# Loading and attending the first row in two halves, in a fused attention and squared-ReLU kernel

## Chip, cores and metric

One core of one Trainium2 chip. The metric is the device time of one execution in microseconds (us), lower is better; the profiled span, which the stages below are read from, is 2 to 3 us shorter than the time. The granted clock is the share of full speed that TensorE was allowed. A run is called slow when it lies over 1.5% above the fastest of the same kernel.

## The reference

```python
# q, k, v: (8 rows, 8 heads, 576 tokens, 64)
rel = pos[:, None] - pos[None, :]
mask_plain = (rel >= 0) & (rel < 32)                        # heads 0..3, "sliding"
mask_dil = (rel >= 0) & (rel < 128) & (rel % 4 == 0)        # heads 4..7, "dilated"
scores = where(mask, scale * q @ k.T, -1e9)
attn_out = softmax(scores) @ v
x = attn_out.transpose(0, 2, 1, 3).reshape(4608, 512)
r = maximum(x @ w_in, 0)                                    # w_in 512 x 2048
return (r * r) @ w_out                                      # w_out 2048 x 512
```

## The kernel before

The 4608 tokens go through the two products in nine chunks of 512; eight rows of attention feed them. Chunk 0 is special: its first product (`x @ w_in`) is cut at token 288, so that it can begin while row 0 is still being attended, and row 1 is attended between its matmuls. From chunk 1 on, round `b` runs chunk `b-1` with the attention of row `b` woven in; `pump(n)` issues `n` pieces of the pending products. `idle()` issues small useless matmuls. Row 0 (cut):

```python
    load_sliding_qk(0, (nc.sync, nc.scalar))        # q and k of row 0, one load each
    load_dilated_qk(0)
    ...
    transposes_and_scores(0, idle_and_load)         # its third call loads w_in, in two pieces
    scores_dilated(0, idle)
    ...
    load_sliding_qk(1); load_dilated_qk(1)          # row 1, behind row 0's third value product
    pending.append(mm1_part_gen(0, g0, 0, 288))     # first product of chunk 0, first part
    for a in range(2):
        pump(1); zs.append(av_dilated(0, 1, a))     # the rest of row 0 between its matmuls
    ...
    load_w_out(); pump(1000)
    pending.append(mm1_part_gen(0, g0, 288, TOKC))  # second part, between the pieces of row 1
    ...
    transposes_and_scores(1, lambda: pump(1))
    pending.append(mm2_by_rows_gen(0, g0))          # second product of chunk 0
```

The round of row 2, and the loads that all rounds share:

```python
    for b in range(2, B):
        pending.append(moe_gen(b - 1))
        pump(1)
        if 2 < b < B - 1:
            dk = keep_qk(b + 1)         # q, k of row b+1 as f16 copies, DRAM to DRAM (POOL's queue)
        ...
        for g in range(2):
            s_sliding_x(b, g); pump(5)  # needs QKTx of row b
        if b == 2:
            cast_v(nc.scalar)           # v of row 2: f32 buffers sv, sd -> f16 vp, vd
            load_v(b + 1)               # v of row 3 into the same sv, sd (SP's queue)
        s_dilated(b, 0); pump(...)
        s_dilated(b, 1)                 # needs QKTd of row b
        if b + 1 < B:
            transpose_by_dma(dk)        # DMA transposes: QKTx, QKTd of row b+1 (SP's queue)
        ...
        attn_values(b, lambda: pump(2))
```

The softmax here doesn't subtract the row's maximum and nothing guards it: scores larger than these inputs give would overflow.

## Time and profile before

| | before |
|---|---|
| time, median of 3 runs | 312.74 us (311.5 to 315.88) |
| profiled span | 310.6 us |
| first product of chunk 0 starts (on 288 tokens) | 22.9 |
| second product of chunk 0 starts | 44.8 |
| chunk 1 starts | 64.0 |
| chunk 2 starts | 99.0 |
| chunk 3 starts | 129.9 |

The starts are those of the first matmul of each stage in the timeline of TensorE. The prediction below shows the lines of chain, timeline and windows that it rests on.

```profile
98.64 0.77 POOL L394 DMA_DIRECT2D out_dram<-otl  x1 [24.20 <-DVE otl L429]
101.19 0.53 POOL L184 DMA_DIRECT2D dk<-in_k_dram  x1
```

The order: v of row 3, then the DMA transposes of row 3, all issued by 98.3 us; only then a burst on the other queue: the last stores of chunk 1 and the copies of q and k of row 4.

### The profile page before, as it was taken

To read this page: it belongs to the slowest core of one execution; us is meant where nothing else is said; L and a number is where in the kernel's file an instruction comes from. 1 tells how busy PE (TensorE), PEld (TensorE's weight loads), DVE (VectorE), ACT (ScalarE), POOL (GpSimd) and SP (SyncE) were. 2 spreads that over 40 slices of the span, in tenths; PEclk is the share of its full clock that TensorE was granted. 3 is DMA by queue.
4 is the path that set the end of the run, shared out by engine and by line. 5 is a ranking of instruction groups with operands and counts; after the bars stand their busy time and mean duration, and the time that the engine had idled before them with its cause. 6 is when DMAs were issued, how large, how long until landed. Compare 5 with 4: busy or idle time off the path is not lost.

```text
span 310.6 us, 7040 instructions
## 1 busy us (share of the span) xinstructions
PE 295.0 (95%) x2920; PEld 197.2 (63%) x2920; DVE 213.5 (69%) x428; ACT 182.5 (59%) x317; POOL 37.3 (12%) x70
## 2 busy tenths in 40 slices
PE   6787999999799999999999999999999999999995
PEld 2666774444487459745984598459845984685484
DVE  5594762679577597759775987598749874834744
ACT  2776883678825982498249824982498236505610
POOL 4340302015001200120012001200100010000000
PEclk9999999999899999999999999999999999999999
DMA  7999899899999999399929992999330003003004
GB/s 182 243 214 243 132 192 233 177 222 285 227 203 158 309 198 190 71 249 222 180 65 256 200 214 46 263 196 180 80 124 0 2 9 128 2 0 138 0 0 137
DMA packets 83312, 47.91 MB, mean 154 GB/s; under 512 B 67792, under 2 KB 79568, under 8 KB 82896
## 3 DMA queue, kind: packets, MB, share of 16 engines
q1 hardware_dynamic: 75060, 26.12, 44.1%
q0 software_dynamic: 6848, 19.80, 28.2%
q10 hardware_dynamic: 1372, 1.54, 1.9%
q8 instruction: 23, 0.38, 0.5%
q14 instruction: 9, 0.07, 0.1%
HBM read 39.85 MB, written 16.52 MB: 181 GB/s over the span
## 4 chain that ended last, share of the span: by engine, by line
PE 75%; DMA 11%; ACT 7%; SPq 2%; issue 2%; DVE 1%; POOL 0%; ACTq 0%; DVEq 0%
PE ph L324 31%; PE poa L374 9%; PE pob L374 9%; DMA wi<-in_moe_w_in_dram 6%; PE pod L374 5%; PE poc L374 4%; PE poe L374 3%; DMA sv<-in_v_dram 3%; ACT vd L145 3%; ACT vp L145 3%; DMA sq<-in_k_dram 2%; SPq L106 2%; PE paw L621 2%; PE pav L607 2%; PE ph L302 2%
## 5 line engine op out<-in xcount | busy, mean ns | idle before, releaser
L324 PE MATMUL ph<-xT,wi 128*128 128x512 f16 x512 | 116.5, 379 | 0.6 <-ACT rt L290 0.6
L290 ACT ACTIVATE rt<-ph 128x512 f16<-128x512 f32 x128 | 73.3, 603 | 20.2 <-PE ph L324 19.8
L324 PEld LDWEIGHTS <-wi 128*128 128x128 f16 x512 | 48.1, 98 | 56.4 <-issue 1.8
L294 DVE TENSOR_TENSOR g<-rt 128x1024 f16<-128x1024 f16 x56 | 38.7, 690 | 36.5 <-ACT rt L290 36.2
L374 PEld LDWEIGHTS <-sm 128*128 128x128 f16 x512 | 46.9, 98 | 4.9
L374 PEld LDWEIGHTS <-g 128*128 128x128 f16 x384 | 36.4, 99 | 7.7 <-DVE g L292 1.3
L374 PE MATMUL poa<-wo,g 128*128 128x256 f16 x256 | 33.4, 278 | 0.2 <-DVE g L294 0.2
L374 PE MATMUL pob<-T,sm 128*128 128x256 f16 x256 | 32.5, 272 | 0.0
L642 ACT COPY xT<-px 128x576 f16<-128x576 f16 x16 | 10.2, 640 | 26.6 <-PE px L636 26.6
L660 ACT COPY xT<-py 128x576 f16<-128x576 f16 x16 | 10.2, 639 | 25.8 <-PE py L654 25.6
L394 POOL DMA_DIRECT2D out_dram<-otl x6 | 4.5, 757 | 162.0 <-DVE otl L429 162.0
L590 DVE TENSOR_TENSOR x_d<-paw,rcp_d 72x512 f16<-72x512 f32 x32 | 22.0, 686 | 1.1
L528 ACT ACTIVATE AT<-pz 128x576 f16<-128x576 f32 x32 | 19.0, 656 | 2.2 <-PE pz L575 1.8
L528 ACT ACTIVATE AT<-ps 128x576 f16<-128x576 f32 x32 | 19.2, 658 | 0.4
L302 PE MATMUL ph<-xT,wi 128*128 128x288 f16 (+1 forms) x128 | 16.8, 272 | 2.1 <-DMA wi<-in_moe_w_in_dram 1.3
L529 DVE TENSOR_TENSOR AT<-AT,maskd 128x576 f16<-128x576 f16 x32 | 14.2, 462 | 6.3 <-ACT AT L528 5.3
L529 DVE TENSOR_TENSOR AT<-AT,maskp 128x576 f16<-128x576 f16 x32 | 14.5, 456 | 3.9 <-ACT AT L528 2.7
L590 DVE TENSOR_TENSOR x_p<-pav,rcp_p 96x512 f16<-96x512 f32 x24 | 16.5, 687 | 0.8
L374 PE MATMUL pod<-T,g 128*128 128x256 f16 x128 | 16.8, 279 | 0.0
L374 PE MATMUL poc<-T,sm 128*128 128x256 f16 x128 | 16.2, 272 | 0.0
L374 PE MATMUL poe<-wo,sm 128*128 128x256 f16 x128 | 16.1, 273 | 0.0
L345 PE MATMUL po<-wo,g 128*128 128x512 f16 x64 | 16.1, 379 | 0.0
(99 smaller groups left out, 359.2 us busy)
## 6 DMA issues: line engine op xcount, KB each, us to landing
sv<-in_v_dram SPq DMA_DIRECT2D x40, 128.0 KB, 10.1
sd<-in_v_dram SPq DMA_DIRECT2D x7, 512.0 KB, 6.3
dk<-in_k_dram POOLq DMA_DIRECT2D x12, 288.0 KB, 7.8
dk<-in_q_dram POOLq DMA_DIRECT2D x12, 288.0 KB, 8.9
out_dram<-otl POOLq DMA_DIRECT2D x6, 512.0 KB, 3.6
out_dram<-otu POOLq DMA_DIRECT2D x6, 512.0 KB, 4.9
wi<-in_moe_w_in_dram POOLq DMA_DIRECT2D x2, 1024.0 KB, 14.1
wo<-in_moe_w_out_dram POOLq DMA_DIRECT2D x4, 512.0 KB, 10.1
```

The source lines that it names most:

```text
L145: nc.scalar.copy(o, i)
L290: nc.scalar.activation(rt[:, o, :], ph[:], ACTF.Relu)
L294: nc.vector.tensor_mul(g[:, ffc - 1 : ffc + 1, :], rt, rt)
L302: nc.tensor.matmul(ph[:, 0 : t1 - t0], wi[:, dmk, ffc * P : ffc * P + P], xs[:, dmk, :], start=(dmk == 0), stop=(dmk == NDM - 1),)
L324: nc.tensor.matmul(ph, wi[:, dmk, ffc * P : ffc * P + P], xs[:, dmk, :], start=(dmk == 0), stop=(dmk == NDM - 1),)
L345: nc.tensor.matmul(po, g[:, ffc, t * P : (t + 1) * P], wo[:, ffc, :], start=(ffc == 0), stop=(ffc == NFF - 1),)
L374: nc.tensor.matmul(acc, lhs[:, k, t * P : (t + 1) * P], rhs[:, k, :], start=(first and k == 0), stop=(k == NK - 1), skip_group_check=True,)
L528: nc.scalar.activation(AT[:, u, 0:UW], ps[:, :, 0 : UW // 2], ACTF.Exp, scale=scale)
L529: nc.vector.tensor_mul(AT[:, u, 0:UW], AT[:, u, 0:UW], mask)
L590: nc.vector.tensor_tensor(out=x[0:w], in0=pv[:, :, :, 0:D], in1=rcp[0:w].unsqueeze(3).to_broadcast([w, 2, HH, D]), op=ALU.mult,)
L642: nc.scalar.copy(xT[:, 0:2, t0 : t0 + 288], px[:, 0:UW].rearrange("x (c t) -> x c t", c=2),)
L660: nc.scalar.copy(xT[:, 2:4, t0 : t0 + 288].rearrange("x c (i r) -> x c i r", r=DIL), py[:, 0:UW].rearrange("x (c r i) -> x c i r", c=2, r= ...
```

## The change

Intent: start row 0 on half of its bytes, so that attention begins while the other half is under way; give w_in in four pieces, w_out behind it in the same queue; and run the first product of chunk 0 on all 512 tokens at once. With row 0 finished before the product, row 1's q and k are loaded later and row 1's transposes and scores stand after the product with nothing between them. The last hunk moves casts and loads of v behind the dilated scores in the round of row 2. The diff, cut to its core:

```diff
-    load_sliding_qk(0, (nc.sync, nc.scalar))
+    load_sliding_qk_half(0, 0, nc.sync)             # tokens 0..287 of q, then of k
+    load_sliding_qk_half(1, 0, nc.scalar)
-    load_dilated_qk(0)
+    load_dilated_qk_half(0)
+    ...  # v for half 0, then q, k and v for half 1
     def load_w_in():
-        for f0, f1 in ((0, 1024), (1024, 2048)):
+        for f0, f1 in ((0, 512), (512, 1024), (1024, 1536), (1536, 2048)):
-    idle_matmuls(pj, 14, TOKC)
+    idle_matmuls(pj, 8, TOKC)
-    def idle():  idle_matmuls(pj, 5, P)
+    def idle(n=3):  idle_matmuls(pj, n, P)
-    transposes_and_scores(0, idle_and_load)
-    scores_dilated(0, idle)
-    ...
+    ...  # casts, transposes, scores, values of half 0, then the same for half 1
+    load_dilated_qk(1)
+    load_w_out()
+    ...
-    pending.append(mm1_part_gen(0, g0, 0, 288))     # with the end of row 0 between
-    ...
-    pending.append(mm1_part_gen(0, g0, 288, TOKC))  # with row 1 between
+    pending.append(mm1_gen(0, g0))
+    pump(18)
+    load_sliding_qk(1)
+    pump(8)
+    cast_sliding_qk(1, ...)
+    pump(1000)
-    transposes_and_scores(1, lambda: pump(1))
-    scores_dilated(1, lambda: pump(3))
+    transposes_and_scores(1, lambda: None)
+    scores_dilated(1, lambda: None)
+    reload_v(1)                                     # moved to behind row 1's scores
@@ the round of row 2 (the last hunk)
             for _ in weight_sums():
                 pump(2)
+            pump(3)
         ...
-        if b == 2:
-            cast_v(nc.scalar)
-            load_v(b + 1)
         s_dilated(b, 0)
         pump(5 if b == 2 else 7)
         s_dilated(b, 1)
+        if b == 2:
+            pump(3)
+            cast_v(nc.scalar)
+            load_v(b + 1)
         if b + 1 < B:
             transpose_by_dma(dk)
-        pump(4 if b == 2 else 9)
+        pump(2 if b == 2 else 9)
```

## The prediction

> **What bounds the kernel now.** I read the page first, then the chain of work that ended last, then the timeline from 0 to 100 us, then the windows. The last 210 us need little reading: the chain there is matmul after matmul.
>
> ```profile
> 129.72 1.48 ACT vp L145
> ...
> 254.80 13.81 PE ph L324 x64
> 268.61 1.75 PE poa L374 x16
> ```
>
> The middle line gives the unit: 64 matmuls of 512 columns in 13.81 us, 0.216 us each. A chunk of the MoE without attention beside it is 26.0 us (254.80 to 280.84), a chunk with a row of attention is 31.2 us (the vp cast opens each round: 129.72, 160.91, 192.11). The change touches nothing after the second chunk (chunk 1), so the question is when chunk 1 starts and how long it takes. Chunk 2 starts at 99.15 in the chain; from there to the end, 211.5 us, I leave as it is. The chain of the first 100 us:
>
> ```profile
> 0.74 7.57 DMA sq<-in_k_dram
> ...
> 12.54 17.23 DMA wi<-in_moe_w_in_dram
> 29.81 4.87 PE ph L302 x40
> ...
> 43.39 10.26 DMA sv<-in_v_dram
> 53.79 1.48 ACT vp L145
> ...
> 64.16 7.36 PE ph L324 x34
> ```
>
> It names loads: q and k of row 0, w_in, then v of row 1. Chunk 1 starts at 64.0. But a chain that names a DMA does not say that TensorE stood still for it. The timeline does:
>
> ```profile
> 22.86 0.42 PE L302 MATMUL ph<-xT,wi 128*128 128x288 f16 x2
> ...
> 27.13 0.63 ACT L660 COPY xT<-py 128x576 f16<-128x576 f16 x1
> ...
> 29.80 5.28 PEld L302 LDWEIGHTS <-wi 128*128 128x128 f16 x47 [1.59 <-DMA wi<-in_moe_w_in_dram]
> ...
> 53.79 1.47 ACT L145 CAST vp<-sv 128x1536 f16<-128x1536 f32 x1 [4.26 <-DMA sv<-in_v_dram]
> ```
>
> Chunk 0 starts at 22.86 on 288 tokens, before row 0 is finished (27.76, the end of the last xT copy). TensorE then loses 1.3 us to w_in and, after 54.6, 0.3 us to v. Its needed work from 22.86 to 64.0 is two products of 13.8 us, about 7.2 us for row 1 (5.1 from 31.2 minus 26.0, and 2.1 for its 48 transposes at 0.43 us per six minus overlap) and some 3 us of the rest of row 0: 37.8 of 41.1 us. So the start is already well packed. The other loss is inside chunk 1, which takes 35.15 us (64.0 to 99.15) where 31.2 is normal:
>
> ```profile
> 80.84 0.30 PE L575 MATMUL pz<-QKTd 64*128 64x72 f16 x8 [1.43 <-ACT AT L528]
> ...
> 84.00:85.00 1.00, 1.00 (x9) 0.76 (x8) 0.99 (x2) 0.00 (x0) 0.00 (x0) 0.50 1.14 243
> ```
>
> The exponentials stand behind 3.5 us of v casts on ScalarE (76.89 to 80.14), TensorE idles from 79.4, and from 83 to 86.3 it runs at clock 0.50.
>
> **What the Trainium skill says.** "TensorE: Matmul & The Clock Gate", section "What's actually happening": the array runs at half clock after an idle window of about 3.4 us and gets full clock back after a busy one. The trace agrees: after 79.4-81.6 with little work the clock reads 0.50 for 3.3 us. The same page, section "Wait — 56ns, not 53.3ns?": 215.7 ns between 512-column matmuls; the trace has 215.8. Its table at the top has ScalarE and VectorE as strict first-in-first-out; the trace agrees with the exponentials held behind the casts. "DMA: Bandwidth & Descriptors", section "Queues, rings and completion order": each DMA engine takes turns between the queues that have work. The trace agrees: k of one row landed 7.6 us after issue at the start and 13.2 us when w_in ran beside it.
>
> **The change, step by step.**
>
> 1. *Earlier first half.* Half of q and k is half the bytes. Before, they landed at 7.6 to 8.3, at 1.5 MB moved in all (rates of the windows summed). Half of that is moved at about 5.1. But VectorE's set-up ends at 5.4 before and gains a larger memset (128x640 for 128x64, about +0.6 us by the 0.27 us of the 128x256 one), so its cast starts near 6.0, not 8.34. Gain here: 2.3 us.
>
> 2. *Two chains in series.* The work of ScalarE and VectorE stays the same in sum (same 576-wide exponentials and masks; VectorE 15.2 us: casts 2x0.95, copies 3.2, masks 8x0.46, normalizations 2.9+3.6). I walk half 0 with the durations before. Cast 6.0-6.95; six transposes and the second six to 7.6; copy 0.64 on ScalarE to 8.0; scores, ready 8.4; exponential to 9.0; k copies (2x0.35) to 9.7; second exponential to 10.3, mask to 10.8; q copies (2x0.41) to 11.6; dilated scores, two exponentials to 13.25, masks to 13.7; normalizations (0.9 and 0.55) to 15.2; VectorE's cast of half 1 only then, to 16.15. Half 1 runs the same chain, with the two dilated normalizations of half 0 in VectorE's order: first exponential to 18.2, second to 19.7 (its bank waits for a normalization), q copies to 21.0, dilated exponentials to 22.65, masks to 23.1, four normalizations to 26.35, eight transposes and the xT copy to 27.4. So row 0 is finished at about 27.4, against 27.76 before with 3 us of MoE matmuls in between. The earlier load is eaten by running the latency chain twice.
>
> 3. *First product undivided.* It needs all of row 0, so it starts at 27.4, not 22.86. w_in is then there: row 0 is 3.4 MB and w_in 2.1 MB landed, 5.5 MB, reached at 25.5 us by the windows' rates. The wait of 1.3 us goes. 64 matmuls: end at 41.2. ScalarE saves 2.7 us (16 of 0.60 for 32 of 0.41 and 0.36), off the path.
>
> 4. *Row 1's q and k.* Their load is behind a memset after four squarings: 27.4 + 8x0.864 + 1.4, about 35.7 (20.9 before). With w_out (2.1 MB) and the dilated half (0.6 MB) nearly through, 1.2 MB at 0.25 MB/us plus 1.8 us land at about 42. The casts stand on ScalarE before the last three ReLUs. Both the ReLUs and the copies follow: casts to 43.9, ReLUs to 45.5, squaring to 45.9, copies of QKT to 47.4.
>
> 5. *Row 1's transposes and scores stand alone.* Before, matmuls filled each step; now nothing does. By the same walk: scores 47, exponentials to 48.2, q/k dilated copies to 49.5, exponentials to 50.1, last copies to 51.4, last dilated scores at 52.3. So mm2 starts at 52.3; in before it started at 44.8. TensorE has some 4 us of work in those 11, so I expect half clock after it: 3.4 us at half speed, about +1.7.
>
> 6. *v of row 1* is loaded behind the last mask, about 53.9, and lands in about 9 us (rows of 0.26 KB; row 2 had 66.9 to about 76). mm2 has 34 matmuls (7.3 us) ahead of it, so the wait is about 0.5.
>
> 7. Chunk 1 starts at 52.3 + 13.8 + 3.6 (values of row 1) + 1.7 + 0.5 = 71.9, against 64.0: **+7.9**.
>
> 8. *v casts of row 2 moved behind the second pair of dilated scores.* This mends the stall of chunk 1: 35.15 to about 31.7: **-3.5**. QKT of row 2 must be there at 71.9 + 8.6 + 0.4 = 80.9; dk starts at 63, 8.7 us, two transposes 7.2 us: 79. Just in time.
>
> Sum: +7.9 - 3.5 = +4.4, a span of 315 us. The time runs about 2 us above the span (312.74 and 310.6): 317. Against my own walk stands that it is hand work of 60 steps and that such a change was presumably made to gain; I take 316.2.
>
> **Rivals.** (a) *DMA bound, and a better order pays.* DMA share is near or over 1 through the first 70 us, so one queue with w_in ahead of w_out may bring everything sooner. If the half chains overlapped more (row 0 at 24.5) and q and k of row 1 landed before the first product ended, steps 4 to 6 would shrink: mm2 at about 46.5, chunk 1 at 64.5, and the gain of step 8 would stand: 309 to 310. For it: the chain names loads for most of the first 54 us. Against it: TensorE's wait for those loads was under 2 us in all there, apart from the first load, and VectorE's 15.2 us after 6.0 plus the tail forbid row 0 before about 22.5.
> (b) *New wait: v and dk of row 2 too late.* dk is held until w_out and v of row 1 have landed. If v is late by 3 us, QKT is missed in chunk 1 and TensorE stalls and cools again: 320 to 322. For it: the slack in step 8 is only 2 us.
> (c) *Clock.* Each idle() now has 3 matmuls for 5, and none in row 1's part. If the first product also starts at half clock, +1.7: 318.
>
> **Range and chances.** Low end: (a) in part, 310. High end: (b) and (c), 322. Faster by over 2% means below 306.5, with chunk 1 starting at 61 or earlier: 34.8 us of TensorE work after row 0 would need row 0 at 26 and no exposed step; I give 0.08. Slower by over 2% is above 319: 0.29. Within: 0.63.
>
> **What would show it.** Right: first 512-column matmul of chunk 0 at 26-28 us, no wait for w_in; sq of row 1 issued at 34-37 and landing at 40-44 with ScalarE waiting for it; a stretch of 5 us or more between the two products of chunk 0 with TensorE mostly idle and clock 0.5 behind it; mm2 starting after 49; chunk 1 at 31-33 us without the wait of 1.43. Wrong: chunk 0 before 25, or mm2 before 47, or TensorE waiting on w_in in pieces, or chunk 1 still over 34.

## More of the kernel before

Timeline of the kernel before, engine SP, then POOL; columns are start, duration, engine, line, operation, out<-in, count, and in brackets the idle time before it. SPq is SP's sequencer, which issues DMAs; dk are the f16 copies of q and k in DRAM, QKTx and QKTd (sliding and dilated heads) their transposes, which the scores read:

```profile
78.38 7.39 SPq L106 DMA_DIRECT2D sv<-in_v_dram  x6
86.95 8.51 SPq L194 DMA_TRANSPOSE QKTx<-dk  x2
95.56 2.72 SPq L196 DMA_TRANSPOSE QKTd<-dk  x2
```

## The result, and the profile after

The kernel after took 342.4 us (median of 4 runs, 339.33 to 351.39, of which the longest is slow), the kernel before 312.28 us beside it. The ratio is 1.0907, with a 95% interval of 1.0779 to 1.1036: slower by 9%. Here and below a ratio is the mean time of one kernel's fast runs over that of the other's of the same rounds, so it isn't quite the ratio of the medians. The range was 310 to 322; the measured time lies 20 us above its end.

| stage (us) | before | after | difference | predicted |
|---|---|---|---|---|
| start to chunk 1 | 64.0 | 76.8 | +12.8 | +7.9 |
| chunk 1 | 35.0 | 32.4 | -2.6 | -3.5 |
| chunk 2 | 30.9 | 50.4 | +19.5 | 0 |
| chunk 3 to the end | 180.7 | 180.6 | -0.1 | 0 |
| span | 310.6 | 340.2 | +29.6 | +4.4 |

Two thirds of the loss are in a stage that the prediction had set aside. The page shows both places at one glance. These are the row for TensorE of the page of before, then the rows for TensorE and for the bytes moved of the page of after, each in 40 equal slices of the span:

```profile
PE   6787999999799999999999999999999999999995
```

```profile
PE   5699958999999504999999999999999999999995
GB/s 179 241 207 204 158 112 2 187 139 199 256 246 222 162 118 167 220 126 22 240 202 195 123 221 216 103 187 222 196 77 105 2 2 123 2 0 126 0 2 123
```

TensorE has two holes: a shallow one in the sixth slice (42 to 51 us) and a deep one in the 14th to 16th (111 to 136 us). In the seventh slice (51 to 60 us) the DMA engines move 2 GB/s: no load is issued until row 1's scores are through (v of row 1, at 58.5).

**The start.** Timeline of the kernel after, TensorE but for the third and fourth lines (SP, ScalarE):

```profile
12.15 0.64 PE L583 MATMUL pg<-ident,early 72*128 72x72 f16 x8 [1.19 <-DMA early<-in_q_dram]
30.10 15.44 PE L358 MATMUL ph<-xT,wi 128*128 128x512 f16 x64
40.49 0.41 SPq L100 DMA_DIRECT2D sq<-in_k_dram  x1
47.32 1.56 ACT L166 CAST early<-sq 96x768 f16<-96x768 f32 x2 [3.74 <-DMA sq<-in_k_dram]
48.21 0.43 PE L533 MATMUL pt<-ident,early 96*128 96x96 f16 x6 [2.67 <-ACT early L166]
57.20 9.05 PE L379 MATMUL po<-wo,g 128*128 128x512 f16 x34
76.81 8.80 PE L358 MATMUL ph<-xT,wi 128*128 128x512 f16 x40
```

The product starts at 30.1, not at the 27.4 of the walk; q and k of row 1 are issued at 40 and wanted at 43.6; TensorE stands 2.7 us for them; row 1 alone takes from 48.2 to 57.2.

**Chunk 2.** Timelines of SP, POOL and TensorE of the kernel after, to set against SP and POOL of before above:

```profile
96.86 5.31 SPq L125 DMA_DIRECT2D sv<-in_v_dram  x6
103.35 10.01 SPq L222 DMA_TRANSPOSE QKTx<-dk  x2
113.46 19.09 SPq L224 DMA_TRANSPOSE QKTd<-dk  x2
```

```profile
108.43 0.77 POOL L428 DMA_DIRECT2D out_dram<-otl  x1 [17.27 <-DVE rcp_d L676]
110.90 0.53 POOL L212 DMA_DIRECT2D dk<-in_k_dram  x1
```

```profile
132.67 0.67 PE L626 MATMUL ps<-QKTx 64*128 64x96 f16 x12 [16.97 <-DMA QKTx<-dk]
```

v of row 3 is now issued 18.5 us later (78.38 to 96.86), 12.8 of which are the later start. Being behind it in SP's queue, the transposes are issued 16.4 us later and now lie under the burst of POOL's queue. Counted from the start of chunk 1, they go out 3.6 us later than before (26.5 for 23.0) and the copies 3.1 us earlier (34.1 for 37.2), since chunk 1 itself is shorter: the lead of the transposes over the copies falls from 14.2 us to 7.6. The chain of the kernel after puts it in one line:

```profile
108.82 23.81 DMA QKTx<-dk
```

A transpose issued at 108.8 lands 23.8 us later, and TensorE stands 17.0 us for it. The DMA view (kind, count, KB each, median us from issue to landing) says who else suffered. Before, 76 to 104 us, and then after, 95 to 135 us:

```profile
dk<-in_k_dram POOLq DMA_DIRECT2D x2, 288.0 KB, 6.8
QKTx<-dk SPq DMA_TRANSPOSE x2, 7.0
```

```profile
dk<-in_k_dram POOLq DMA_DIRECT2D x2, 288.0 KB, 18.3
QKTx<-dk SPq DMA_TRANSPOSE x2, 16.3
```

Both sides of the overlap take over twice as long, and so does the second store of chunk 1 (17.0 us for 5.0). And the engines moved little in that time; windows of the kernel after (busy time by engine, then granted clock, DMA share, GB/s):

```profile
116.00:120.00 4.00, 0.00 (x0) 0.00 (x0) 0.69 (x1) 0.34 (x1) 0.00 (x0) 0.80 0.51 40
...
124.00:128.00 4.00, 0.00 (x0) 0.00 (x0) 0.00 (x0) 0.00 (x0) 0.00 (x0) 0.50 1.36 127
```

40 and 127 GB/s in the two windows shown, 158 in the one between them, against 257 in the 4 us ahead of them. So the bandwidth that these engines had just shown was not used up; whether the transfers hinder one another is tested below (e3). When TensorE gets its operand it has idled long enough to be at clock 0.50.

### The profile page after: what moved, and what is told of

It is laid out like the page before. It is cut to its first block, busy times and chain, and to the rows that moved or that the text cites. A ratio compares the mean times of both kernels' runs of the same rounds, so it can differ in the third digit from the quotient of the medians.

```text
span 340.2 us, 6812 instructions
## 1 busy us (share of the span) xinstructions
PE 304.3 (89%) x2816; PEld 197.0 (58%) x2816; DVE 214.6 (63%) x420; ACT 180.5 (53%) x299; POOL 45.4 (13%) x75
## 3 DMA queue, kind: packets, MB, share of 16 engines
q1 hardware_dynamic: 75460, 26.12, 40.5%
## 4 chain that ended last, share of the span: by engine, by line
PE 68%; DMA 13%; ACT 8%; SPq 4%; DVE 3%; issue 2%; POOL 0%; ACTq 0%; DVEq 0%; POOLq 0%
PE ph L358 31%; PE poa L408 8%; PE pob L408 7%; DMA QKTx<-dk 7%; PE poc L408 4%; PE pod L408 4%; ACT vp L166 3%; PE poe L408 3%; DMA early<-in_q_dram 3%; SPq L125 2%; PE paw L710 2%; DMA sq<-in_k_dram 2%; ACT vd L166 2%; PE po L379 2%; SPq L222 2%
## 5 line engine op out<-in xcount | busy, mean ns | idle before, releaser
L358 PE MATMUL ph<-xT,wi 128*128 128x512 f16 x576 | 133.3, 385 | 1.5 <-ACT rt L324 1.2
L324 ACT ACTIVATE rt<-ph 128x512 f16<-128x512 f32 x144 | 82.7, 603 | 26.9 <-PE ph L358 26.4
L358 PEld LDWEIGHTS <-wi 128*128 128x128 f16 x576 | 55.0, 99 | 66.8 <-issue 6.5
L328 DVE TENSOR_TENSOR g<-rt 128x1024 f16<-128x1024 f16 x63 | 43.5, 691 | 51.4 <-ACT rt L324 51.1
L408 PE MATMUL poa<-wo,g 128*128 128x256 f16 x256 | 32.3, 273 | 0.0
L626 PE MATMUL ps<-QKTx 64*128 64x96 f16 x144 | 5.4, 210 | 17.0 <-DMA QKTx<-dk 17.0
L379 PE MATMUL po<-wo,g 128*128 128x512 f16 x64 | 17.3, 408 | 0.0
L677 DVE TENSOR_TENSOR x_p<-pav,rcp_p 96x512 f16<-96x512 f32 (+1 forms) x25 | 16.6, 665 | 0.9
L626 PEld LDWEIGHTS <-QKTx 64*128 64x128 f16 x144 | 3.7, 98 | 22.0 <-issue 22.0
L408 PE MATMUL poe<-wo,sm 128*128 128x256 f16 x128 | 16.3, 273 | 0.0
```

The source lines that it names most:

```text
L324: nc.scalar.activation(rt[:, o, :], ph[:], ACTF.Relu)
L328: nc.vector.tensor_mul(g[:, ffc - 1 : ffc + 1, :], rt, rt)
L358: nc.tensor.matmul(ph, wi[:, dmk, ffc * P : ffc * P + P], xs[:, dmk, :], start=(dmk == 0), stop=(dmk == NDM - 1),)
L379: nc.tensor.matmul(po, g[:, ffc, t * P : (t + 1) * P], wo[:, ffc, :], start=(ffc == 0), stop=(ffc == NFF - 1),)
L408: nc.tensor.matmul(acc, lhs[:, k, t * P : (t + 1) * P], rhs[:, k, :], start=(first and k == 0), stop=(k == NK - 1), skip_group_check=True,)
L626: nc.tensor.matmul(ps[:, e, QB * j : QB * (j + 1)], QKTx[r, 1, q0 - PADP : q0 - PADP + P], QKTx[r, 0, q0 : q0 + QB], start=True, stop=True,)
```

## The experiments

Twelve kernels ran, all with correct results. The theory after the first look: (A) the last hunk pushes the transposes of row 3 into the burst, and the copies of row 4 slow them: some 17 us; (B) the start loses through its longer chain, the late loads of row 1 and the unfilled row 1. The rivals are named with each run. Starts in us from the profiled run of each; times are medians and ranges of all runs of a kernel, ratios of the fast ones:

| run | time | ratio to before | first product | chunk 1 | chunk 2 | chunk 3 |
|---|---|---|---|---|---|---|
| before | 312.3 | 1 | 22.9 | 64.0 | 99.0 | 129.9 |
| after | 342.4 | 1.091 | 30.1 | 76.8 | 109.2 | 159.6 |
| e1 transposes first | 338.1 | 1.084 | 27.7 | 74.7 | 107.0 | 155.9 |
| e2 last hunk undone | 327.1 | 1.052 | 28.4 | 74.6 | 110.4 | 141.2 |
| e3 copies of row 4 held | 325.5 | 1.044 | 29.6 | 75.4 | 107.8 | 143.8 |
| e4 before plus hunk | 318.1 | 1.017 | 24.0 | 63.3 | 95.7 | 133.9 |
| e5 before plus hunk, held | 311.3 | 0.997 | 23.7 | 63.0 | 95.4 | 129.0 |
| e6 e2, row 1 loaded early | 323.2 | 1.036 | 29.5 | 72.3 | 108.1 | 139.2 |
| e7 e6, row 1 filled | 320.4 | 1.027 | 29.4 | 68.6 | 106.1 | 137.0 |
| e8 before, undivided | 313.3 | 1.008 | 25.8 | 64.1 | 99.1 | 130.0 |
| e9 before, w_in in four | 311.6 | 1.002 | 25.2 | 65.0 | 99.9 | 130.7 |
| e10 halves, divided | 316.1 | 1.016 | 21.2 | 65.7 | 101.7 | 132.5 |
| e11 e7, more idle matmuls | 324.6 | 1.043 | 29.1 | 67.6 | 110.8 | 141.7 |
| e12 before, half of the hunk | 311.0 | 0.999 | 23.6 | 63.3 | 96.1 | 127.0 |

From chunk 3 to the end they all take about 181 us, so the difference between two kernels is that between their last columns.

### e1_transposes_first: the after kernel with the transposes ahead of v

```diff
         if b == 2:
             pump(3)
+            transpose_by_dma(dk)
             cast_v(nc.scalar)
             load_v(b + 1)
-        if b + 1 < B:
+        elif b + 1 < B:
             transpose_by_dma(dk)
```

> The changed kernel with one thing moved: in round b=2 the four DMA transposes of row 3 are issued ahead of the v loads of row 3, everything else as changed. Theory 1 (the late transposes meet the chunk-1 stores and the dk copy of row 4 and are slowed to 24 us): the transposes go out near 95 us, land before 112, the 17 us wait of the scores of row 3 for QKTx goes, time 342 - 19 = 321 to 324 us. Rival (the transposes are slow for a cause of their own, such as the state of the DMA rings after a late start): wait of over 8 us stays, time above 332.

Measured: 338.07 us (337.68 to 338.46), ratio 1.084 (1.0812 to 1.0868). Far above what was expected. The wait for QKTx is gone, yet another of the same size stands in chunk 2. Timeline of this run, SP, then ScalarE, then TensorE:

```profile
107.64 8.79 SPq L125 DMA_DIRECT2D sv<-in_v_dram  x6
...
122.01 1.47 ACT L166 CAST vp<-sv 128x1536 f16<-128x1536 f32 x1 [14.15 <-DMA sv<-in_v_dram]
...
127.11 3.31 PE L358 MATMUL ph<-xT,wi 128*128 128x512 f16 x8 [16.02 <-ACT rt L324]
```

The transposes, issued at 99.2, now land in 5 to 6 us, but v of row 3 is issued behind them, from 107.6 to 119.4, across the burst. ScalarE was free for its cast from 107.9 on and gets v only at 122.0; the cast stands ahead of the ReLUs, and TensorE waits 16.0 us for those. What the two kernels share is that all of SP's loads for row 3 are issued after the dilated scores, shortly before the burst; which one is late depends on the order. How much of this wait is the burst and how much only the late issue, no run takes apart: the copies themselves took no longer here than before (6.8 us).

### e2_last_hunk_undone: the after kernel with the round of row 2 as before

The edit is the last hunk of the diff above, backwards.

> The changed kernel with its last hunk undone: the v casts and v loads of round b=2 stand again ahead of the dilated scores, as in the kernel before. Theory 1: chunk 1 is long again (about 35 us, was 32.4), but the transposes of row 3 go out about 10 us after the v loads and clear of the stores, chunk 2 about 31 us: 342 - 19.5 + 2.8 = 325 us. Rival (the stall of chunk 2 comes from the late start of the whole pipeline, not from the hunk): the wait stays, time above 335.

Measured: 327.05 us (323.65 to 330.56), ratio 1.0524 (1.0459 to 1.059). As expected: chunk 1 takes 35.8 us and has its stall back, chunk 2 takes 30.9 and has no wait for QKTx. So the hunk, on top of this start, costs some 15 us net (342.4 - 327.1). Of what is left, the profiled run, the fastest of the four, has 10.6 us ahead of chunk 1; where the two other fast runs lose 3 us more isn't on record.

### e3_dk4_held: the after kernel with the copies of row 4 held back

```diff
+        if b == 3:
+            for i in range(2):     # POOL reads the ends of QKTx and QKTd of row 3 first
+                nc.gpsimd.tensor_copy(hold, QKTx[:, i, ...])
+                nc.gpsimd.tensor_copy(hold, QKTd[:, i, 1, ...])
         if 2 < b < B - 1:
             dk = keep_qk(b + 1)
```

> The changed kernel with the DRAM copy of q and k of row 4 held back until the transposes of row 3 have landed; the stores of chunk 1 still go out beside the transposes. If it is the dk copy that slows the transposes: QKTx of row 3 lands near 115 to 118 us for 132.7 and the time falls by 12 to 17 us, to 325 to 330. If the stores slow them: little change, over 336. If the transposes are slow alone: no change.

Measured: 325.54 us (2 runs), ratio 1.0438 (1.0393 to 1.0483). Transposes and stores stay where the change had put them; only the four copies wait. Timelines of TensorE and POOL, then two lines of the DMA view (95 to 125 us):

```profile
116.60 0.44 PE L626 MATMUL ps<-QKTx 64*128 64x96 f16 x12 [2.29 <-DMA QKTx<-dk]
...
120.36 0.52 POOL L212 DMA_DIRECT2D dk<-in_k_dram  x1
```

```profile
dk<-in_k_dram POOLq DMA_DIRECT2D x2, 288.0 KB, 7.1
QKTx<-dk SPq DMA_TRANSPOSE x2, 9.5
```

And the line of its chain to set against the 23.81 us above:

```profile
108.62 7.94 DMA QKTx<-dk
```

As expected. The same transpose, issued at the same time, lands after 7.9 us instead of 23.8; the wait falls from 17.0 to 2.3 us, the transposes from 16.3 to 9.5, the copies from 18.3 to 7.1. So the copies are what turned the delay into a stall; the stores of chunk 1 alone, still beside the transposes, do not. Chunk 2 still takes 36.0 us for 30.9 before: the rest of the delay stays. Why a copy from DRAM to DRAM and a transpose that reads DRAM hinder one another so much is not shown by these runs.

### e4_before_plus_hunk and e5_before_hunk_dk4_held: the hunk on the kernel before

e4 is the last hunk alone on the kernel before, e5 the same with the hold of e3.

> The kernel before with the last hunk of the change alone. Theory 1: chunk 1 falls from 35.2 to about 32.4 us, then the transposes of row 3 meet stores and the dk copy as in the changed kernel and chunk 2 loses 10 to 20 us: 320 to 329 us. Rival (the hunk is harmless, the stall needs the late start): 309 to 310 us, a gain of about 3.

> The kernel before with the last hunk, and with the dk copy of row 4 held until the transposes of row 3 have landed. If the collision with the dk copy is the whole cost of the hunk, chunk 1 stays near 32.1 us (35.2 before), chunk 2 is 31 to 33 us, and the time is 308.5 to 310.5: faster than both kernels by under 1%. If v of row 3 or row 4 comes late instead, chunk 2 or 3 is over 34 us and the time is 313 or more.

Measured: e4 318.14 us (315.62 to 320.55), ratio 1.0174 (1.0104 to 1.0244); e5 311.31 us (310.22 to 311.92, 6 runs), ratio 0.9974 (0.9945 to 1.0003). Alone, the hunk does what it was made for: chunk 1 takes 32.4 us in both, against 35.0. But in e4 chunk 2 takes 38.2. That is 7.3 us more than before, where 10 to 20 were expected, and the time is below the 320 to 329 expected: slower, though not clearly by 2%. Timeline of TensorE in e4:

```profile
103.57 0.44 PE L556 MATMUL ps<-QKTx 64*128 64x96 f16 x12 [1.33 <-DMA QKTx<-dk]
```

There is a further wait of 3.2 us for QKTd. The collision is there on the kernel before too, only smaller. The traces show one difference of place: in e4 both of QKTx's transposes are issued by 97.7, as the copies begin (97.4), in after only by 113.4, across the copies (110.9). With the copies held (e5) chunk 2 takes 33.6, where 31 to 33 were expected: the gain in chunk 1, 2.6 us, is all but spent again. 0.26% less time is within the interval of none.

### e8_before_undivided: the undivided product alone on the kernel before

```diff
-    pending.append(mm1_part_gen(0, g0, 0, 288))
-    ...  pump(1) between the last pieces of row 0
+    ...  idle() between the last pieces of row 0
+    pending.append(mm1_gen(0, g0))
+    pump(14)
-    pending.append(mm1_part_gen(0, g0, 288, TOKC))
```

> The kernel before with one part of the change alone: the first product of chunk 0 is undivided and starts when all of row 0 is attended; row 0 is still loaded whole, row 1's scores still stand between its matmuls. Theory 2a (undividing costs because TensorE does nothing useful while row 0 finishes): the first product starts at 26 to 27 us for 22.9, chunk 1 at 66.5 to 68 for 64.0, time +3 to +4: 314.5 to 315.5. Rival (the fewer ReLUs and the end of the wait for w_in pay it back): chunk 1 within 1 us of 64, 311 to 313.

Measured: 313.34 us (312.53 to 317.12), ratio 1.0082 (1.0024 to 1.014). Here my reading fell: the product starts 3 us later (25.8) and the second product nonetheless at 44.6 (44.8 before), chunk 1 at 64.1. The wait for w_in is gone, and 64 matmuls of 512 columns took the place of 128 shorter ones. So on a whole row undividing delays nothing by the start of chunk 1 in this profile. Over the runs the kernel is still 0.8% slower (0.2 to 1.4%); the profiled run was the fastest of the four, and where the others lose is not on record.

### e6_row1_qk_early and e7_row1_qk_early_filled: row 1

e6 is e2 with q and k of row 1 issued during the second half of row 0; e7 is e6 with row 1 woven into the first product again.

```diff
     ys += av_dilated(0, 0, 1)
+    nc.vector.memset(sq[:, :, :, 0:1], 0.0)
+    load_sliding_qk(1)
     ...
     pump(18)                                  # e7: pump(10) for this and the next pump
-    nc.vector.memset(sq[:, :, :, 0:1], 0.0)
-    load_sliding_qk(1)
     pump(8)
     cast_sliding_qk(1, ...)
 e7 alone
-    pump(1000)
+    pump(4)
-    transposes_and_scores(1, lambda: None)
-    scores_dilated(1, lambda: None)
+    transposes_and_scores(1, lambda: pump(1))
+    scores_dilated(1, lambda: pump(2))
+    pump(1000)
```

> The changed kernel with the last hunk undone (chunk 1 began at 74.8 us there), and q and k of row 1 loaded as soon as their staging buffer is free (about 21 us) instead of behind nine groups of the first product. Theory 2b (the late load is a part of the lost time): the casts find their data, the stretch between the two products shrinks by 2.5 to 4 us, chunk 1 begins at 71 to 72.5, time 3 us less than 327. Rival (the early load delays w_in): TensorE waits on w_in in the first product, chunk 1 at 74 or later.

> As the run with the early load of row 1, and the transposes and scores of row 1 stand between the matmuls of the first product, as in the kernel before, instead of alone after it. Theory 2c (the unfilled chain, and the half clock behind it, is the largest part): chunk 1 begins at 64 to 67 us, time 316 to 319. Rival (the loads bind, so that the fill only moves the wait): chunk 1 at 70 or later.

Measured: e6 323.21 us (ratio 1.0358, 1.0294 to 1.0422), e7 320.37 us (1.0267, 1.0212 to 1.0321), two runs each. Chunk 1 starts at 72.3 and then 68.6, after 74.6 in e2: 2.3 us for the late load, 3.7 us for the unfilled row 1. The first product happened to start 1.1 us later in e6 than in e2; from its start to the second product, after, e1, e2 and e3 take 26.2 to 27.3 us, e6 23.0 and e7 19.4, so the late load is rather worth 3 to 4 us. e7 was expected at 64 to 67 and fell short.

### e10_halves_divided and e11_more_idle_matmuls: what is left of the start

e10 is e7 with the first product cut at 288 tokens again, its first part between the pieces of the second half; e11 is e7 with more idle matmuls.

```diff
 e10
+    pending.append(mm1_part_gen(0, g0, 0, 288))   # behind half 1's last transposes
     for g in range(2):
         s_dilated_half(1, g)
-        idle()
+        pump(1)                                   # and so at the gaps that follow
     ...
-    pending.append(mm1_gen(0, g0))
+    pending.append(mm1_part_gen(0, g0, 288, TOKC))
 e11
-    idle_matmuls(pj, 8, TOKC)
+    idle_matmuls(pj, 14, TOKC)
-    def idle(n=3):
+    def idle(n=8):
```

> Two halves of row 0 with q and k of row 1 early, the last hunk undone, and the first product divided again at 288 tokens, so that the first part fills the attention of the second half. If the start lost its time because the halves leave TensorE with nothing to do, the first matmul of the first product starts at 22 to 24 us, the first product of chunk 1 at 64 to 67 (72.3 and 68.6 in the two runs before) and the time is 314 to 319. If the loads and the chain of the halves set it whatever fills them, chunk 1 starts at 68 or later and the time is 320 or more.

> As the run with the filled transposes of row 1 (320.4), with 14 idle matmuls ahead of row 0 and 8 instead of 3 at each gap. If half clock in row 0 is what delays it, the granted clock is 1.0 from 8 to 30 us, the first product starts at 27 to 28 us (29.4) and chunk 1 at 66.5 to 67.5 (68.6): 318 to 319. If the chain of casts and loads sets it, the idle matmuls only add to it: start at 29.4 or later, 320 or more.

Measured: e10 316.14 us (two runs, ratio 1.0156, 1.0113 to 1.0199), chunk 1 at 65.7, as expected. The first product starts at 21.2, 1.7 us earlier than in the kernel before, which is what the halves were meant for. Chunk 1 starts 2.9 us earlier than in e7 (65.7 for 68.6), but not all of it is the division: e7 ran the second half of row 0 at half clock and e10 didn't, already before any part of the product stood in it, and that is worth some 1.5 us (see e11). The rest fits the gaps that half 1 leaves TensorE, which only the product of half 0 can fill.

e11: 324.6 us (two runs, ratio 1.0428, 1.0393 to 1.0463). The clock was at 1.00 from 16 us on, and the first product started at 29.1, only 0.3 earlier than in e7. That doesn't clear half clock, though: of the chain from the dilated q to the product 3.4 us are now idle matmuls, 1.3 in e7. Two traces at hand are a cleaner pair. After and e2 are the same code up to the first product, and the dilated q lands at 12.0 in both. Timelines of TensorE in after, whose first product is shown above, then in e2:

```profile
25.24 0.65 PE L693 MATMUL pav<-vp,AT 128*128 128x65 f16 x8
```

```profile
23.96 0.43 PE L693 MATMUL pav<-vp,AT 128*128 128x65 f16 x8
28.42 14.26 PE L358 MATMUL ph<-xT,wi 128*128 128x512 f16 x64
```

By what the same matmuls take, half 1 ran at half speed in after and at full speed in e2 (from 17.7 us on). The product starts at 30.1 and at 28.4, and takes 15.4 and 14.3 us. So half clock costs the start 1.7 us and the product 1.2 more. e1 (27.7) falls on the side of e2, e3 (29.6), e6 and e7 on that of after. This is a part of the loss; the chains to the first product show another. The undivided whole row (e8), then the halves (e11); start, duration, what:

```profile
3.23 10.14 DMA early<-in_q_dram
...
25.98 0.43 PE ph L324 x2
```

```profile
3.46 8.22 DMA early<-in_q_dram
...
16.26 0.69 DVE x_p L677
...
25.45 0.69 DVE x_p L677
...
29.23 1.95 PE ph L358 x9
```

The dilated q, the load that the chain hangs on, lands at 13.4 whole and at 11.7 by halves (12.0 in e2): half the bytes, 1.4 to 1.7 us. From there to the product it is 12.6 us whole and 17.5 us by halves (16.4 in e2). The chain by halves has seven of VectorE's normalizations in it, two of them shown, 4.3 us in all; that of the whole row has three, 2.1 us. In e11 1.7 us are gained and 4.9 paid, but 1.7 of these are its additional idle matmuls on the chain (3.4 us for 1.7); in e2, which has 0.4 us of them there, 1.4 are gained and 3.8 paid.

Why e11 is slower than e7 in the end lies in chunk 1, which takes 43.2 us. Timeline of ScalarE and TensorE in e11:

```profile
91.27 1.04 ACT L166 CAST vd<-sd 128x1024 f16<-128x1024 f32 x1 [5.73 <-DMA sd<-in_v_dram]
...
92.92 0.96 PE L645 MATMUL pz<-QKTd 64*128 64x72 f16 x16 [9.91 <-ACT AT L598]
```

The second piece of the dilated v of row 2 was issued at 79.8 and landed after 11.4 us; the stores of chunk 0 and the copies of row 3 were issued from 78.9 to 82.5. In e7, where POOL's queue had the copies 1.5 us later (82.0 against 80.5), the same load landed after 6.1 us and its cast waited 0.2. That looks like the burst again, one row earlier, but no run here takes it apart.

### e9_before_w_in_four: w_in in four pieces alone

```diff
-        for f0, f1 in ((0, 1024), (1024, 2048)):
+        for f0, f1 in ((0, 512), (512, 1024), (1024, 1536), (1536, 2048)):
```

> The kernel before with w_in in four pieces and nothing else. If the pieces are a gain by themselves, the wait of 1.3 us for w_in at 29.8 us shrinks and the second product starts up to 1.3 us earlier than 44.8: 311 to 312. If they are free, 312 to 313.5. If more issues on the queue push the loads of row 1 later, first product of chunk 1 starts after 64.5 us and the time is 313 or more.

Measured: 311.58 us (311.35 to 313.4), ratio 1.0023 (0.9994 to 1.0052). The wait of 1.28 us for w_in is gone from the timeline, but in the profiled run, the slowest of its four, row 0 was itself 2.3 us late (first product at 25.2), which may be why no wait was left. The pieces change nothing that can be measured.

### e12_before_split_cast: half of the hunk

```diff
         if b == 2:
-            cast_v(nc.scalar)
-            load_v(b + 1)
+            cast_sliding_v(nc.scalar, NB)
+            load_sliding_v(b + 1)
         s_dilated(b, 0)
         pump(5 if b == 2 else 7)
         s_dilated(b, 1)
+        if b == 2:
+            cast_dilated_v(nc.scalar, DIL)
+            load_dilated_v(b + 1, nc.sync)
```

> The kernel before, only in the round of row 2: cast and next load of the sliding v stay where they were, those of the dilated v move behind the second dilated scores, yet ahead of the DMA transposes of row 3. If half the move is enough to mend chunk 1 without pushing the transposes into the burst of stores and of the copy of row 4, chunk 1 takes 32 to 33 us (35.0 before), chunk 2 stays at 30 to 31.5, and the time is 309 to 310.5. If the transposes still meet the copy, chunk 2 takes 33 to 38 us and the time is 312 to 318.

Measured: 310.99 us (median of 6; two runs, 316.02 and 318.79, are slow and not used in the ratio), ratio 0.9986 (0.996 to 1.0012). Timeline of SP in this run:

```profile
77.66 7.11 SPq L106 DMA_DIRECT2D sv<-in_v_dram  x6
...
85.96 7.78 SPq L194 DMA_TRANSPOSE QKTx<-dk  x2
```

The transposes are issued at 86.0, where the kernel before has them (86.95), chunk 1 takes 32.8 us and chunk 2 keeps its 30.9, as expected; the time is 0.5 us above the 309 to 310.5 expected. In the profiled runs that is 2.9 us of span less than before (307.7, 310.6); over the fast runs (309.5 to 311.3) the gain is not distinguishable from none.

## Why the prediction was wrong, point by point

**The step that failed: "Chunk 2 starts at 99.15 in the chain; from there to the end, 211.5 us, I leave as it is."** From the start of chunk 2 to the end the kernel after takes 231.0 us. Step 8 looked at the hunk only for what it takes away in chunk 1. The moved `load_v` is also an entry in SP's queue. It now goes out behind the dilated scores, right ahead of the transposes of row 3, which stood there already and so go out later by the time that it takes. Rival (b), "v and dk of row 2 too late", had the right kind of wait in mind, but one row too early: QKT of row 2 was in time, that of row 3 was not. e2 shows that the hunk is the cause, e3 that the copies of row 4 are what it collides with, e1 that another order in the same place is no better, e4 that it costs on the kernel before as well. Size: +19.5 us in chunk 2.

**The steps of the start, mis-sized.** They add up to +12.8 in place of +7.9. Of the 4.9 us between, 2.7 are in step 2 and 1.6 in step 3, and most of both is half clock (rival (c)) ahead of and in the first product, for which the sum had nothing:

- *Step 1.* VectorE's cast of half 0 began at 5.5, where 6.0 was expected. Right.
- *Step 2*, row 0 finished at 27.4: 30.1 in the profiled run of after, 27.7 to 29.6 in e1 to e3, which have the same start. The walk took the dilated q as there when its turn came (copies done at 11.6); it landed at 12.0 and they were done at 13.7, 2.1 us late. From those copies to the product the walk had 15.8 us, the trace has 16.4, and 14.8 in e2, where half 1 ran at full clock. The mechanism ("The earlier load is eaten by running the latency chain twice") was right, and e2 against e8 puts it at 3.8 us paid for 1.4 gained.
- *Step 3.* No wait for w_in: right. The 64 matmuls took 15.4 us instead of 13.8, the first twelve 4.2 us of them (0.35 each, where 0.216 is normal), the half clock of rival (c); in e2 all 64 took 14.3. Counting the later start of the undivided product as a loss was right by halves (e10, 2.9 us, some 1.5 of it clock) but not as a rule (e8, none by chunk 1).
- *Step 4.* sq issued at 40.5 instead of 35.7 and landed at 47.3 instead of 42: the 2.7 us of step 2 and those of step 3. The late load is worth 2.3 to 4 us (e6).
- *Step 5.* From landing to second product 10.3 us predicted, 9.9 measured; filling it is worth 3.7 (e7).
- *Steps 6 and 7.* Second product to chunk 1, 13.8 + 3.6 + 1.7 + 0.5 = 19.6 predicted, 19.6 measured. The 1.7 for half clock is there: the first 34 matmuls take 9.05 us, 7.3 at 0.216 each.

The shares of the +12.8 can be read only roughly, as each run has one profile and half clock alone moves chunk 1 by some 2 us (after against e2). From the runs one after the other: 2.2 between after and e2, whose code is the same up to there (clock, no effect of the code); 2.3 late load (3 to 4 from the first product on); 3.7 unfilled row 1; 2.9 undivided product on halves, some 1.5 of it clock; 1.7 left in e10, in which the halves, the pieces of w_in and the fewer idle matmuls are not told apart. They are read in that order, and in another they could divide differently.

**Step 8** itself: chunk 1 at 31.7 predicted, 32.4 measured. Right in kind, mis-sized by 0.7. (The v casts hold ScalarE for 3.25 us there, 76.89 to 80.14; the 3.5 of the prediction adds up records that overlap.)

**Chances.** Slower by over 2% had 0.29. Its two grounds, (b) and (c), were additions of at most 6 us to the sum; nothing in the working could have reached 342. So the direction of the start was foreseen by reasoning; that of chunk 2 was not foreseen at all.

What stays open: why the copies and the transposes slow each other to 40 to 158 GB/s, and why TensorE came to full speed in the second half of row 0 in e1, e2 and e10 and not in after, e3, e6 and e7, all with three idle matmuls at a gap. The start of the product, 27.7 to 30.1 us in kernels that share that code, follows from it for the larger part.

## What to carry to other kernels

When a load is moved for the sake of the buffer or engine it blocks, follow it into its queue: everything behind it moves too, and the question is what the other queues issue at that time. Halving a load pays only if what it releases is long against the chain of dependent steps that now runs twice; here half the bytes came 1.4 us earlier and the chain cost 3.8 (e2 against e8). And work without a dependency on the critical chain (here the first product beside row 1's scores, 3.7 us in e7) is worth most exactly where the chain leaves gaps, so it shouldn't be taken out of them in the same change that makes the gaps.

## What the Trainium skill lacked or had wrong

- "DMA: Bandwidth & Descriptors", section "Rules for kernel authors", says that a DMA transpose next to ordinary DMAs needs nothing. That is about correctness, and all results here were correct; but what the two cost each other is on no page. Beside four copies from DRAM to DRAM of 288 KB each, a transpose took 23.8 us at worst and 16.3 at the median to land, the copies 18.3; with the copies held back 9.5 and 7.1 (e3).
- "TensorE: Matmul & The Clock Gate", section "Seeing it yourself", warns that the clock events in a trace can be unreliable. In the kernel after the windows give clock 1.00 from 24 to 28 us, in e7 0.50, yet the same eight matmuls (pav, L693) take 0.65 us there in both, and 0.42 in e11 at full clock. Windows of after, then of e7:

```profile
24.00:28.00 4.00, 3.66 (x52) 2.99 (x49) 2.45 (x8) 1.30 (x2) 3.87 (x7) 1.00 1.21 207
```

```profile
24.00:28.00 4.00, 3.66 (x54) 3.22 (x53) 2.96 (x8) 1.05 (x2) 3.25 (x5) 0.50 1.15 269
```

- The same page, section "What's actually happening", gives one busy window of some 3.4 us as enough for full clock. In after, e1, e2 and e3, which share the code up to there, TensorE is busy for 3.5 to 3.7 us of the 4 from 12 to 16 us; e1 and e2 are at full speed from about 17.7 us on, after and e3 only in the first product. What share of a window has to be busy is not on the page, and these runs don't give it either.
- The same section asks for an idle window of some 3.4 us before half clock. In chunk 1 of the kernel before, the stretch that the prediction takes as agreement, the clock is 0.50 from 83.0 on though TensorE was busy for 1.6 of the 3.4 us up to 82.8 and its longest wait was 1.43 us. The matmuls slowed with it: ten of 256 columns take 2.37 us from 82.60 on, eight take 1.03 us at 86.95. Here less than a whole idle window was enough.
